# One load moved up in GpSimd's order: the experts' output weights in a fused attention and mixture-of-experts kernel

## The chip, the core and the metric

The kernel runs on one core of one Trainium2 chip, as one program launched once. A core has five engines that run side by side, each through its own list of instructions in order: TensorE for matrix products (PE in the profile, with its weight loads shown apart as PEld), VectorE (DVE), ScalarE (ACT), GpSimd (POOL) and SyncE (SP). An engine goes on to its next instruction when the semaphores which that instruction waits for have come. Transfers between the chip's main memory and the on-chip memory run on 16 DMA engines. They are issued by an instruction on SP, ACT or POOL, and the issuing engine does not wait for them to land.

The metric is the device time of one execution in microseconds (us), as the median of several runs.

## The reference: what is computed

Four batches of 768 positions with 8 heads of 64 columns go through two stages. The first is a sparse attention: each query sees its neighbours within a window, and 24 block summaries (the maximum of the keys of a block of 32 and the mean of its values). The second is a mixture of four attention experts, of which each position uses two.

```
k_sum = k.reshape(B, H, nb, block, D).max(axis=3)
v_sum = v.reshape(B, H, nb, block, D).mean(axis=3)
...
a = np.exp(scores_all)
a = a / (np.sum(a, axis=-1, keepdims=True) + 1e-09)
v_all = np.concatenate([v, v_sum], axis=2)
return np.matmul(a, v_all).astype(np.float32)
```

```
for e in range(E):
    q = x @ wq[e]
    k = x @ wk[e]
    v = x @ wv[e]
    scores = scale * (q @ k.transpose(0, 2, 1))
    ...
    ye = a @ v @ wo[e]
    for kk in range(K):
        mask = topk[:, :, kk] == e
        out += mask[..., None] * w[:, :, kk:kk + 1] * ye
```

The step of this text is the load of `wo`, the last factor in `a @ v @ wo[e]`.

## The kernel before

The kernel is written as a list of some 770 small steps, made by `make_plan`. Each step has a name, the buffers that it reads and writes, and a function that emits its instructions. No loop and no scheduler sets the order in which they run: a hand-made text, `TABLE` (lines 56 to 110), lists the steps by number. Each entry is a step's number, the engine that runs it (P for TensorE, V, A, G for GpSimd, S for SyncE) and the slots of on-chip buffers that it takes. `emit` walks through the table and emits each step. Since every engine runs its own instructions in the order in which they were emitted, the order of the G entries in the table is GpSimd's order, and so on for each engine. What holds between engines are semaphores alone.

In step names the first digit is the batch. The second is the pair of heads (in the first stage) or the pair of experts (in the second).

First stage, for each of four pairs of heads of a batch:

- `dk`, `dq` (lines 263 and 268) load keys and queries through GpSimd's DMA queue. `dv` (lines 287 to 295) loads the values window by window through SP's queue. `dvs` (line 347) loads them once more by blocks, into the one buffer `vt`, and `tr` (line 355, GpSimd) adds them up to block sums. `hc` (line 300) copies window edges and `ds` (line 363) spreads the sums; both run on GpSimd through the copying helper at line 172, `ds` in places on ScalarE.
- `tk`, `tq` (line 374, TensorE) transpose keys and queries. `kw`, `cq` (ACT or DVE) copy them out. `rk` (line 390, DVE) takes the maximum over blocks, and `ksc` (GpSimd) spreads it into `kw`.
- `sc` (lines 422 and 428, TensorE) are the scores, `ex` (line 435, ACT) their exponentials, `av` (line 445, TensorE) the product with the values, `rc` and `xm` (DVE) the normalisation. `tx`, `hi` and `lo` (lines 471 to 490) transpose the result and split it into two half-precision parts.

Second stage, for each batch:

- `vp` (lines 557 and 560, TensorE) gives the experts' values and the gate's logits. `pp` (line 633) gives queries and keys of one pair of experts.
- `sp` (line 657, TensorE), `es` (line 665, ACT) and `dm` (line 670, GpSimd) are the scores of one block of positions, their exponentials and the causal mask. There are six blocks, 0 to 5, for each pair of experts. `aw` (line 681, TensorE) is the product with the values, in three steps; its first step reads blocks 0, 2 and 4.
- `r2` and `wv` (lines 700 to 707, DVE) weigh it with the gate, `tw` (line 718, TensorE) transposes it, and `ct` copies it into the tile `wT`.
- `op` (line 740, TensorE) multiplies `wT` with the output weights, tile `wo`. `oc` copies the result out of the accumulation banks and `od` stores it.

The output weights are loaded once, by step 146, `dwo`, from 32-bit rows into 16-bit ones:

```
def dwo(e):
    nc.gpsimd.dma_start(out=T["wo"], in_=moe_wo.rearrange("(c e) d n -> (e d) c n", c=2))
R.step("dwo", {"G": 0.72}, [], [wo], dwo, dma=256 * 0.066 / 16)
```

The tile has a buffer of its own that nothing else uses, so this load waits for nothing but its turn on GpSimd. Its first reader is step 222, `op00`, the first `op` step of batch 0. In TensorE's order `op00` follows `sp114`, and `pp101`, `sp111`, `sc210`, `tk23` and `tk22` come behind it.

GpSimd's order around the load is, before the change: `dm013`, `dm010`, `dm015`, `dm014`, `dm011`, `dk300`, `dm000`, `dm012`, `dm002`, `dk210`, `dm003`, `dm001`, `dm005`, `tr300`, `dm004`, `dq210`, `ksc20`, `tr301`, `dm110`, **`dwo`**, `vone1` (five small fills, lines 212 to 216), `hc21`, `dm112`, `hc33`, `hc20`, `dm113`, `dm114`, `dq300`, `dm111`, `dm115`, `hc23`, `tr210`, `ksc23`, `ksc22`, `tr211`, `dm101`.

Of the kernel before, what the change touches and what calls it, by code (L numbers as in the profile page):

```python
# [15 lines left out]
S = 768  # L16
# [55 lines left out]
154,P,6 158,V, 271,V, 159,A, 314,P,2.2 155,V, 156,V, 414,G,0 206,P,0 315,A, 295,P,4.3 166,P,6.0 207,A, 160,V,2.0  # L72
162,V, 161,A, 316,P,0.1.0 167,A, 163,V, 317,P, 416,G, 587,S,0 296,A, 585,S, 168,P,6.0 586,S, 318,V, 171,P,2 588,S,
169,A, 319,V, 299,P,4.0.1 415,G, 300,P, 172,A, 180,P,0 419,S,2 301,V, 320,P,6.6.6 208,G, 181,A, 302,V, 199,G,
452,P,2.0 214,G, 435,P,3.2 321,V, 453,A, 205,G, 177,P,4 303,P,0.7.7 211,G, 579,G,1 448,P,2.1.2 436,A, 322,V, 597,S,0
178,A, 170,G, 431,P,3.0.1 202,G, 183,P,6 304,V, 173,G, 184,A, 174,P,4 417,G,0 449,A, 365,P,6.1 305,V, 179,G, 182,G,
175,A, 433,V, 185,G, 367,P,0.0 589,G, 366,A, 450,V, 432,A, 215,P,0.0.4 368,V, 217,P, 421,S,3 451,A, 216,P, 176,G,
372,P,6.1 218,V, 418,G,2 378,P,2 373,A, 186,P,1.1.0 434,G, 219,V, 188,P, 590,G,1 379,A, 187,P, 369,P,6 189,V,
437,P,4.5 370,A, 190,V, 326,P,2.1.1 438,A, 191,P,6.0 327,V, 456,P,0.1 371,G, 328,A, 423,S,0 192,V, 220,P,4.1 146,G,
426,S, 457,A, 221,V, 439,P,2.4 424,S, 375,P,6 38,G,1 440,A, 384,P,4 425,S, 222,P,0.0 376,A, 338,P,2.2 223,V, 408,G,  # L80
385,A, 381,P,6 339,A, 224,S, 454,P,4.2 374,G, 598,G, 482,P,0.2.0 465,P,1.0.2 382,A, 484,V, 329,P,2 455,A, 406,G,
467,V, 323,P,6 483,A, 331,V, 380,G, 377,G, 330,V, 336,P,4.0 466,A, 324,V, 332,V,0.1 580,G,0 334,V, 333,A, 325,A,
383,G, 228,P,2.2 386,G, 337,A, 335,V, 422,G, 225,P,6.4 229,A, 346,P,4.0 427,G, 226,V, 349,P,0 347,A, 387,P,1.0.2
389,P, 350,A, 227,S, 352,P,6 230,S, 388,P, 353,A, 340,P,4 390,V, 485,G, 469,P,0.1 468,G, 391,V, 607,P,1.1.1 341,A,
459,P,6.1.2 428,G,0 470,V, 608,A, 392,P,2.0 458,P, 393,V, 355,P,4 609,V, 473,P,2.3 356,A, 486,P,0.2 474,A, 442,P,4.0.0
460,V, 354,G, 461,V, 600,S,0 487,A, 348,G, 441,P, 601,S, 342,G, 430,G, 343,P,2 443,V, 471,P,0.0 344,A, 472,A, 444,V,
628,P,6.0 624,P,7.0.0 629,V, 357,G, 490,P,4.1 610,G, 462,P,2.0.0 488,P,0.2 491,A, 345,G, 625,V, 351,G, 611,P,6.1
# [817 lines left out]
```

## Time and profile before

| What | us |
|---|---|
| median of 3 runs | 172.43 (171.61 to 174.34) |
| the profiled execution, its own time | 172.59 |
| its span, first to last instruction | 170.9 |
| TensorE busy, of the span | 147.0 (86%) |
| ScalarE busy | 122.2 (72%) |
| VectorE busy | 113.6 (66%) |
| GpSimd busy | 111.1 (65%) |

The span leaves out 1.69 us of the execution's own time (172.59 - 170.9), which lies before its first and behind its last instruction. The profile's page cuts the span into 40 equal slices of 4.27 us and gives a digit for each engine and slice, the busy share in tenths. The row PEclk gives in the same way the clock that TensorE was granted, and the row DMA the load of the 16 DMA engines. The chain of waits is followed back from the last instruction, at each step to what released it. In a timeline a row gives the start, the duration, the engine, the line, the operation, its tiles and the number of instructions merged into it, and in square brackets how long the engine had been idle and what ended that. The ends of matrix products are modelled, so neighbouring rows of TensorE overlap a little. A letter q behind an engine's name marks its sequencer, which issues transfers.

### The profile page before, as it was taken

How to read it: one execution, taken by the hardware profiler on the slowest of the kernel's cores; microseconds unless marked ns; L12 is line 12 of the kernel's file. 1: busy time of each engine (PE TensorE's matmuls, PEld its weight loads, DVE VectorE, ACT ScalarE, POOL GpSimd, SP SyncE). 2: the span in 40 equal slices, each digit the busy share in tenths (PEclk: the TensorE clock that was granted, in tenths of full speed). 3: DMA queues.
4: the chain of work that ended last, by engine and by line, in shares of the span. 5: the costliest groups of instructions: out<-in, count | busy, mean ns of one | idle time of the engine just before them, and what ended most of it. 6: DMA issues, size and time to landing. Idle time of an engine off the chain costs nothing.

```text
span 170.9 us, 6961 instructions
## 1 busy us (share of the span) xinstructions
PE 147.0 (86%) x2993; PEld 107.9 (63%) x2993; DVE 113.6 (66%) x237; ACT 122.2 (72%) x154; POOL 111.1 (65%) x185
## 2 busy tenths in 40 slices
PE   0099999999999999910799998899999999899795
PEld 0076878777867777810265787865777886466552
DVE  5646899897967598710237688893778777546750
ACT  3058989687759898960069978958989795899650
POOL 7988579997789999999029868508799430116000
PEclk9999999999999999995579999999999999999999
DMA  3999999999899699994730370899910000030546
GB/s 26 225 203 230 164 180 206 204 209 205 176 157 202 120 165 211 218 222 104 98 123 0 141 204 4 109 215 190 351 71 4 4 4 2 4 123 0 203 181 233
DMA packets 44222, 24.31 MB, mean 142 GB/s; under 512 B 33184, under 2 KB 40864, under 8 KB 43808
## 3 DMA queue, kind: packets, MB, share of 16 engines
q1 hardware_dynamic: 35824, 16.27, 42.4%
q0 software_dynamic: 7824, 6.56, 26.0%
q10 hardware_dynamic: 544, 1.05, 1.6%
q8 instruction: 23, 0.38, 1.0%
q14 instruction: 7, 0.06, 0.1%
HBM read 24.13 MB, written 6.29 MB: 178 GB/s over the span
## 4 chain that ended last, share of the span: by engine, by line
PE 64%; DMA 11%; POOL 10%; DVE 6%; issue 3%; SPq 2%; ACT 2%; DVEq 0%; POOLq 0%; ACTq 0%
PE ps L633 12%; PE ps L445 11%; PE ps L740 7%; PE ps L557 6%; DMA vb<-in_v_dram 6%; DMA wo<-in_moe_wo_dram 5%; PE ps L681 5%; PE ps L657 4%; PE ps L374 4%; PE ps L471 3%; PE ps L422 3%; POOL vt L355 3%; POOL a L670 3%; PE ps L312 2%; PE ps L428 2%
## 5 line engine op out<-in xcount | busy, mean ns | idle before, releaser
L665 ACT ACTIVATE a<-ps 128x1024 f16<-128x1024 f32 (+1 forms) x48 | 42.1, 922 | 5.4 <-PE ps L657 5.0
L670 POOL TENSOR_SCALAR_AFFINE_SELECT a<-a 128x256 f16<-128x256 f16 x48 | 18.5, 407 | 30.7 <-ACT a L665 30.1
L435 ACT ACTIVATE aT<-ps 120x768 f32<-120x768 f32 x32 | 25.2, 811 | 8.3 <-PE ps L428 7.2
L445 PE MATMUL ps<-vb,aT 120*64 120x65 f32 x768 | 26.2, 223 | 0.7 <-DVE rec L456 0.4
L445 PEld LDWEIGHTS ps<-vb,aT 120*64 120x64 f32 x768 | 23.9, 138 | 3.6 <-issue 1.1
L172 POOL COPY vb<-vb 32x1408 f32<-32x1408 f32 x14 | 18.8, 1349 | 9.8 <-DMA vt<-in_v_dram 6.4
L633 PE MATMUL ps<-hi,wqk 128*128 128x384 f16 x128 | 24.4, 338 | 0.5 <-issue 0.3
L170 ACT COPY kw<-ps 128x1152 f16<-128x1152 f16 x13 | 14.5, 1134 | 8.4 <-PE ps L374 7.7
L355 POOL TENSOR_TENSOR vt<-vt 120x1024 f32<-120x1024 f32 (+3 forms) x16 | 19.2, 1199 | 1.8 <-DMA vt<-in_v_dram 0.9
L740 PE MATMUL ps<-wo,wT 128*128 128x512 f16 (+1 forms) x50 | 12.7, 391 | 8.8 <-DMA wo<-in_moe_wo_dram 8.8
L390 DVE TENSOR_REDUCE ks<-ps 128x24 f16<-128x768 f16 x16 | 14.9, 948 | 6.5 <-ACT kw L170 3.4
L633 PEld LDWEIGHTS <-wqk 128*128 128x128 f16 x128 | 12.4, 101 | 9.9 <-issue 2.8
L170 ACT CAST qk<-ps 128x768 f16<-128x768 f32 x10 | 8.1, 809 | 13.7 <-PE ps L633 13.7
L490 DVE TENSOR_TENSOR lo<-ps,hi 128x768 f16<-128x768 f32 x16 | 15.2, 954 | 2.1 <-ACT hi L170 1.7
L374 PE MATMUL ps<-idr,kn 100*64 100x100 f16 x256 | 8.9, 219 | 8.4 <-DMA kn<-in_k_dram 8.3
L460 DVE TENSOR_TENSOR x<-ps,rec 128x768 f32<-128x768 f32 x16 | 15.3, 956 | 0.5
L657 PE MATMUL ps<-qk,qk 64*128 64x512 f16 (+3 forms) x128 | 14.9, 311 | 0.7 <-ACT qk L170 0.4
L557 PE MATMUL ps<-wvg,hi 128*128 128x264 f16 x96 | 13.8, 275 | 0.1
L172 DVE COPY ob<-ps 128x1024 f32<-128x1024 f32 (+2 forms) x5 | 4.7, 957 | 13.7 <-PE ps L740 13.7
L374 PEld LDWEIGHTS <-kn 100*64 100x64 f16 x256 | 7.3, 117 | 9.3 <-DVE vb L216 8.2
L740 PEld LDWEIGHTS <-wT 128*128 128x128 f16 x50 | 4.4, 100 | 13.9 <-DMA wo<-in_moe_wo_dram 8.9
L428 PEld LDWEIGHTS <-kw 64*128 64x128 f16 x384 | 10.5, 99 | 2.8 <-issue 0.7
(99 smaller groups left out, 292.0 us busy)
## 6 DMA issues: line engine op xcount, KB each, us to landing
vb<-in_v_dram SPq DMA_DIRECT2D x32, 176.0 KB, 5.7
out_dram<-ob SPq DMA_DIRECT2D x9, 512.0 KB, 3.4
vt<-in_v_dram SPq DMA_DIRECT2D x16, 192.0 KB
kn<-in_k_dram POOLq DMA_DIRECT2D x8, 192.0 KB, 6.2
qn<-in_q_dram POOLq DMA_DIRECT2D x8, 192.0 KB, 5.3
kn<-in_k_dram POOLq DMA_DIRECT2D x4, 384.0 KB, 7.5
qn<-in_q_dram POOLq DMA_DIRECT2D x4, 384.0 KB, 6.5
out_dram<-ob ACTq DMA_DIRECT2D x2, 512.0 KB
```

Of the source, the lines that this page charges most:

```text
L170: nc.scalar.copy(dst, src)
L172: en(e).tensor_copy(dst, src)
L355: en(e).tensor_tensor(y[0:120], x[0:120, 0:w], x[0:120, w:2 * w], AL.add)
L374: nc.tensor.transpose(dst[64 * hp:64 * hp + 64, p * s:p * s + p], src[:, hh + hp, 64 * s:64 * s + 64], idt)
L435: nc.scalar.activation(T["aT"][aT.slot][0:KR], pbank(sc, 2)[0:KR, :, 0:384], AF.Exp, scale=SCALE)
L445: nc.tensor.matmul(pbank(av, 2)[o:o + 64, u, 65 * (2 * (t // 2) + hp):65 * (2 * (t // 2) + hp) + 65], a[0:KR, hp, 64 * t:64 * t + 64], T[" ...
L557: nc.tensor.matmul(p[:, i, 0:264], hi_(ch)[:, cols], T["wvg"][:, ch, :], start=(ch == 0), stop=False, skip_group_check=True)
L633: nc.tensor.matmul(pbank(pp, 2)[:, u, 0:384], T["wqk"][:, cc, ch, j, :], hi_(ch)[:, 384 * u:384 * u + 384], start=(ch == 0), stop=(ch == N ...
L657: nc.tensor.matmul(pbank(sp, 2)[:, ep, c0:c0 + w], T["qk"][qk[1].slot][r, 128 * tj:128 * tj + 128], T["qk"][qk[0].slot][r, n0:n0 + w], sta ...
L665: nc.scalar.activation(a2v(u), pbank(sp, 2)[:, :, 0:ln], AF.Exp, scale=SCALE / (XS * XS))
L670: nc.gpsimd.affine_select(m, m, [[0, 2], [1, 128]], AL.is_ge, 0.0, base=0, channel_multiplier=-1)
L740: nc.tensor.matmul(pbank(op, i1 - i0)[:, ti - i0, 0:n1 - n0], T["wT"][wTs[cc].slot][:, 128 * ti:128 * ti + 128], T["wo"][:, cc, n0:n1], st ...
```

## The change

Entry `146,G` is taken out of its place in the table, behind `dm110` (371) and `220,P`, and put in behind `dm014` (205). GpSimd so issues the load ahead of fifteen entries of its order that it followed before: twelve that compute and the three loads `dk300`, `dk210` and `dq210`, which use the same DMA queue. The order of all other entries, on every engine, stays as it was; the other changed lines of the diff are the same entries with other line breaks.

```
-452,P,2.0 214,G, 435,P,3.2 321,V, 453,A, 205,G, 177,P,4 303,P,0.7.7 211,G, 579,G,1 448,P,2.1.2 436,A, 322,V, 597,S,0
...
-437,P,4.5 370,A, 190,V, 326,P,2.1.1 438,A, 191,P,6.0 327,V, 456,P,0.1 371,G, 328,A, 423,S,0 192,V, 220,P,4.1 146,G,
-426,S, 457,A, 221,V, 439,P,2.4 424,S, 375,P,6 38,G,1 440,A, 384,P,4 425,S, 222,P,0.0 376,A, 338,P,2.2 223,V, 408,G,
...
+452,P,2.0 214,G, 435,P,3.2 321,V, 453,A, 205,G, 146,G, 177,P,4 303,P,0.7.7 211,G, 579,G,1 448,P,2.1.2 436,A, 322,V,
...
+437,P,4.5 370,A, 190,V, 326,P,2.1.1 438,A, 191,P,6.0 327,V, 456,P,0.1 371,G, 328,A, 423,S,0 192,V, 220,P,4.1 426,S,
+457,A, 221,V, 439,P,2.4 424,S, 375,P,6 38,G,1 440,A, 384,P,4 425,S, 222,P,0.0 376,A, 338,P,2.2 223,V, 408,G, 385,A,
```

More of the change, by code (lines that the diff above doesn't have):

```diff
@@ L74 @@
 169,A, 319,V, 299,P,4.0.1 415,G, 300,P, 172,A, 180,P,0 419,S,2 301,V, 320,P,6.6.6 208,G, 181,A, 302,V, 199,G,
-452,P,2.0 214,G, 435,P,3.2 321,V, 453,A, 205,G, 177,P,4 303,P,0.7.7 211,G, 579,G,1 448,P,2.1.2 436,A, 322,V, 597,S,0
-178,A, 170,G, 431,P,3.0.1 202,G, 183,P,6 304,V, 173,G, 184,A, 174,P,4 417,G,0 449,A, 365,P,6.1 305,V, 179,G, 182,G,
-175,A, 433,V, 185,G, 367,P,0.0 589,G, 366,A, 450,V, 432,A, 215,P,0.0.4 368,V, 217,P, 421,S,3 451,A, 216,P, 176,G,
-372,P,6.1 218,V, 418,G,2 378,P,2 373,A, 186,P,1.1.0 434,G, 219,V, 188,P, 590,G,1 379,A, 187,P, 369,P,6 189,V,
@@ L79 @@
-437,P,4.5 370,A, 190,V, 326,P,2.1.1 438,A, 191,P,6.0 327,V, 456,P,0.1 371,G, 328,A, 423,S,0 192,V, 220,P,4.1 146,G,
-426,S, 457,A, 221,V, 439,P,2.4 424,S, 375,P,6 38,G,1 440,A, 384,P,4 425,S, 222,P,0.0 376,A, 338,P,2.2 223,V, 408,G,
-385,A, 381,P,6 339,A, 224,S, 454,P,4.2 374,G, 598,G, 482,P,0.2.0 465,P,1.0.2 382,A, 484,V, 329,P,2 455,A, 406,G,
-467,V, 323,P,6 483,A, 331,V, 380,G, 377,G, 330,V, 336,P,4.0 466,A, 324,V, 332,V,0.1 580,G,0 334,V, 333,A, 325,A,
-383,G, 228,P,2.2 386,G, 337,A, 335,V, 422,G, 225,P,6.4 229,A, 346,P,4.0 427,G, 226,V, 349,P,0 347,A, 387,P,1.0.2
@@ L84 @@
-389,P, 350,A, 227,S, 352,P,6 230,S, 388,P, 353,A, 340,P,4 390,V, 485,G, 469,P,0.1 468,G, 391,V, 607,P,1.1.1 341,A,
+452,P,2.0 214,G, 435,P,3.2 321,V, 453,A, 205,G, 146,G, 177,P,4 303,P,0.7.7 211,G, 579,G,1 448,P,2.1.2 436,A, 322,V,
+597,S,0 178,A, 170,G, 431,P,3.0.1 202,G, 183,P,6 304,V, 173,G, 184,A, 174,P,4 417,G,0 449,A, 365,P,6.1 305,V, 179,G,
+182,G, 175,A, 433,V, 185,G, 367,P,0.0 589,G, 366,A, 450,V, 432,A, 215,P,0.0.4 368,V, 217,P, 421,S,3 451,A, 216,P,
+176,G, 372,P,6.1 218,V, 418,G,2 378,P,2 373,A, 186,P,1.1.0 434,G, 219,V, 188,P, 590,G,1 379,A, 187,P, 369,P,6 189,V,
@@ new lines @@
+437,P,4.5 370,A, 190,V, 326,P,2.1.1 438,A, 191,P,6.0 327,V, 456,P,0.1 371,G, 328,A, 423,S,0 192,V, 220,P,4.1 426,S,
+457,A, 221,V, 439,P,2.4 424,S, 375,P,6 38,G,1 440,A, 384,P,4 425,S, 222,P,0.0 376,A, 338,P,2.2 223,V, 408,G, 385,A,
+381,P,6 339,A, 224,S, 454,P,4.2 374,G, 598,G, 482,P,0.2.0 465,P,1.0.2 382,A, 484,V, 329,P,2 455,A, 406,G, 467,V,
+323,P,6 483,A, 331,V, 380,G, 377,G, 330,V, 336,P,4.0 466,A, 324,V, 332,V,0.1 580,G,0 334,V, 333,A, 325,A, 383,G,
+228,P,2.2 386,G, 337,A, 335,V, 422,G, 225,P,6.4 229,A, 346,P,4.0 427,G, 226,V, 349,P,0 347,A, 387,P,1.0.2 389,P,
@@ L85 @@
+350,A, 227,S, 352,P,6 230,S, 388,P, 353,A, 340,P,4 390,V, 485,G, 469,P,0.1 468,G, 391,V, 607,P,1.1.1 341,A,
 459,P,6.1.2 428,G,0 470,V, 608,A, 392,P,2.0 458,P, 393,V, 355,P,4 609,V, 473,P,2.3 356,A, 486,P,0.2 474,A, 442,P,4.0.0
```

## The prediction

> **What bounds the kernel now.** I read the page's slices first, then its chain of waits.
>
> ```profile
> span 170.9 us, 6961 instructions
> PE   0099999999999999910799998899999999899795
> POOL 7988579997789999999029868508799430116000
> PEclk9999999999999999995579999999999999999999
> PE 64%; DMA 11%; POOL 10%; DVE 6%; issue 3%; SPq 2%; ACT 2%; DVEq 0%; POOLq 0%; ACTq 0%
> ```
>
> TensorE is nine tenths busy nearly everywhere, with one hole in the 18th and 19th slice (72.6 to 81.2 us), and its clock falls right behind that. The question is what the hole is. The list of waits, the two engines' timelines and the chain in time answer it:
>
> ```profile
> PE ps L740 <- DMA wo<-in_moe_wo_dram: 8.8, 1, 8.8
> 73.14 0.47 PE L657 MATMUL ps<-qk,qk 64*128 64x512 f16 x4
> 82.38 1.89 PE L740 MATMUL ps<-wo,wT 128*128 128x512 f16 x4 [8.78 <-DMA wo<-in_moe_wo_dram]
> 72.97 0.73 POOL L520 DMA_DIRECT2D wo<-in_moe_wo_dram  x1
> 72.97 9.37 DMA wo<-in_moe_wo_dram
> ```
>
> GpSimd issues the load at 72.97. TensorE has ended its `sp114` and is at `op00` by 73.60, and waits 8.78 us in program order until the load has landed at 72.97 + 9.37 = 82.34. It is the longest single wait on TensorE in its mid-program.
>
> **The load's new place.** It goes behind four of the five mask steps of the first row below (1.85 us for five, 0.37 each), so it is issued at about 60.47 + 4 x 0.37 = 61.95, and moves up by 11.0 us.
>
> ```profile
> 60.47 1.85 POOL L670 TENSOR_SCALAR_AFFINE_SELECT a<-a 128x256 f16<-128x256 f16 x5
> 62.26 0.71 POOL L263 DMA_DIRECT2D kn<-in_k_dram  x1
> 64.05 0.67 POOL L263 DMA_DIRECT2D kn<-in_k_dram  x1
> 68.12 0.40 POOL L670 TENSOR_SCALAR_AFFINE_SELECT a<-a 128x256 f16<-128x256 f16 x1
> 73.69 0.16 POOL L212 MEMSET vb<- 96x24 f32 x1
> ```
>
> *What is late behind it.* Fifteen entries of GpSimd shift by the issue's 72.97 to 73.69, 0.72 us. From 73.69 on GpSimd stands where it stood, since the same instructions lie before that point. Of the fifteen only one is read at once: `dm004`, the row at 68.12, ends at 68.52, and TensorE's `aw000`, which reads block 4, is the second row of 42 products here:
>
> ```profile
> 68.55 1.45 PE L681 MATMUL ps<-v,a 128*128 128x65 f16 x42
> 72.24 1.07 DVE L172 COPY wT<-ps 128x768 f16<-128x768 f16 x2
> ```
>
> It starts 0.03 us after the mask, so I charge it 0.7 us. Behind `aw000` TensorE's queue holds everything up to `op00`, and `op00` also needs the two copies into `wT`, which VectorE makes after `aw000` and which shift along: they end at 73.31 now, 74.0 then. TensorE reaches `op00` at 73.55 + 0.7 = 74.25. The bounds of this term are 0 (if ScalarE's work ahead of the mask hides it) and 0.73.
>
> *When the load lands.* No row shows it at this place. The nearest are the loads on the same software queue, above all the two `kn` loads that are issued in this stretch now (8.0 in the median), the `wo` load itself (9.4), and a `qn` load on a quiet queue (4.8):
>
> ```profile
> kn<-in_k_dram POOLq DMA_DIRECT2D x2, 384.0 KB, 8.0
> wo<-in_moe_wo_dram POOLq DMA_DIRECT2D x1, 256.0 KB, 9.4
> qn<-in_q_dram POOLq DMA_DIRECT2D x1, 384.0 KB, 4.8
> 64.00:68.00 4.00, 4.00 (x60) 2.90 (x58) 3.63 (x4) 3.90 (x5) 4.00 (x6) 1.00 1.25 209
> ```
>
> So between 61.95 + 4.8 = 66.8 and 61.95 + 9.4 = 71.3; I take 8.0, 70.0. Even the late end is 2.9 us ahead of 74.25: the wait goes entirely.
>
> *Whom the transfer displaces.* At the stretch's 209 GB/s (last number of the window's row), 256 KB are 1.25 us for all that is queued behind. `dk210` lands at 64.05 + 8.0 = 72.1 now, then at 72.1 + 0.72 + 1.25 = 74.0; its reader `tk23` stands at 87.81 now and comes to 77.3 (10.5 earlier, below). Slack is 3.3 us. SP's value loads are delayed as well, but their first readers on GpSimd (`hc33`, `hc23`) come at 76 us and later. This is hidden.
>
> **The clock.** While TensorE waits its granted clock halves, and it works slowly after the wait:
>
> ```profile
> 77.00:78.00 1.00, 0.00 (x0) 0.00 (x0) 0.00 (x0) 0.00 (x0) 1.00 (x2) 0.68 0.73 130
> 82.38:84.27 1.89, 1.89 (x5) 0.73 (x6) 0.00 (x0) 0.00 (x0) 0.00 (x0) 0.50 1.16 177
> 87.40:88.00 0.60, 0.60 (x22) 0.46 (x20) 0.00 (x0) 0.60 (x2) 0.00 (x0) 0.83 0.90 345
> 82.38 1.89 PE ps L740 x4
> 84.27 2.56 PE ps L633 x8
> 91.00 1.32 PE ps L633 x8
> 115.26 0.97 PE ps L740 x4
> ```
>
> The last four rows are of the chain of waits: `op00` took 1.89 where the same four products take 0.97 at 115.26, and `pp101` 2.56 where eight take 1.32 at 91.00. That is 0.92 + 1.24 = 2.16 us. The rest up to about 87.5 (`sp111` and `sc210`, some 1 us in the chain at half clock) can hold at most half of itself more, 0.5; I take 0.24, in all 2.4, with bounds 2.16 and 2.66. Without the wait there is nothing to halve the clock: it held at 1.00 for 3.4 us of idleness here, from 73.6 to 77, and the new gap at `aw000` is 0.7.
>
> The Trainium skill, page "TensorE: Matmul & The Clock Gate", section "Part 1: The HAM clock gate (the "warmup" mystery)", says that an idle window of about 3.4 us halves the clock and about 3.4 us of sustained work restores it. The fall at 77 agrees; the way back does not, since the mean clock rises only within the row from 87.40 on, 5.0 us after the work began. By the page's 3.4 us at half speed the loss would be an estimated 1.7 us, and the sum below 0.7 us smaller; the rows decide.
>
> **The sum.** Span: 170.9 - 8.78 (wait) + 0.7 (`dm004`) - 2.4 (clock) = 160.4. With the 1.69 us around the span (172.59 - 170.9) that is 162.1 us; the profiled execution is 0.16 above the median of the runs (172.43), which I leave out. The gain is 10.5 us, 6%.
>
> **Does it hold to the end?** What used the wait to catch up is next in line: ScalarE and VectorE, idle 11.51 and 11.06 us around it, and GpSimd.
>
> ```profile
> 74.06 1.30 ACT L665 ACTIVATE a<-ps 128x1024 f16<-128x1024 f32 x2
> 86.87 0.80 ACT L170 CAST qk<-ps 128x768 f16<-128x768 f32 x1 [11.51 <-PE ps L633]
> 84.38 1.23 DVE L172 COPY ob<-ps 128x1024 f32<-128x1024 f32 x1 [11.06 <-PE ps L740]
> 80.05 0.77 POOL L268 DMA_DIRECT2D qn<-in_q_dram  x1
> 88.67 0.77 POOL L670 TENSOR_SCALAR_AFFINE_SELECT a<-a 128x256 f16<-128x256 f16 x2 [7.86 <-ACT a L665]
> 94.52 0.66 PE L681 MATMUL ps<-v,a 128*128 128x65 f16 x16
> 103.24 0.77 POOL L670 TENSOR_SCALAR_AFFINE_SELECT a<-a 128x256 f16<-128x256 f16 x2 [1.93 <-ACT a L665]
> 105.54 1.45 PE L681 MATMUL ps<-v,a 128*128 128x65 f16 x42
> ```
>
> ScalarE ends its backlog at 74.06 + 1.30 = 75.36, then 76.1; its next work, the copy behind `pp101`, is ready at 86.87 - 10.4 = 76.5. VectorE is free at 74.0 and `op00` ends at 75.2. Neither is late. GpSimd is: it runs without a gap to 80.82 and begins the row of 88.67 there, only 7.86 us earlier, where TensorE has moved by 10.5. So it is 2.6 us behind its old place relative to TensorE. Its readers have room: `aw110`, the products at 94.52, come to 84.0, and the masks end at 81.6. Further on GpSimd waits 1.93 us at 103.24, which takes the lag down to 0.7 us; the reader at 105.54 has 105.54 - 104.01 = 1.5 us of room. So I let TensorE keep its 10.5 us; the loads for batch 3 are released by TensorE itself and move with it.
>
> **Rivals.**
>
> *GpSimd sets the pace.* If a reader that I have not found stands close behind one of GpSimd's steps between 81 and 93 us, or the block loads for `tr210` land late and stretch them, TensorE keeps only GpSimd's 7.86: 170.9 - 7.86 + 1.69 = 164.7. For it speaks that GpSimd is busy in all the slices of 60 to 80; against it the rooms just counted.
>
> *The load starves at its new place, and nothing is gained.* At 61.95 VectorE is in steady work, at 72.97 it was about to go idle. If GpSimd's transfer could not start beside VectorE, it would begin at VectorE's first long pause, 73.31 + 0.7 = 74.0, and land 9.4 later at 83.4, 1.1 behind 82.34: 172.59 + 1.1 = 173.7, no change by the measurement. The two `kn` loads, issued in just this stretch, landed in 8.0 and took 0.71 and 0.67 to issue, no more than `wo` beside an idle VectorE: that speaks plainly against it. The rule behind it is the Trainium skill's, page "SBUF — State Buffer", the box on the DVE blocking DMA: GpSimd cannot write its transfers' descriptors while VectorE holds a port that both share in certain fast modes. By its example (620 ns alone, 3100 ns beside such a copy) the loss would be an estimated 2.5 us and would stay within the slack of 2.9.
>
> *Slower: the queue is served one load at a time.* All GpSimd loads share one queue. If each load there held up the next for its full 9.4 us, `wo` would land at 71.3, `dk300` at 80.7 and `dk210` at 90.1. TensorE would then wait for keys at `tk23`, in the place of the weights, from 77.3 to 90.1, and lose its clock again: 162.1 + 12.8 + 2.4 = 177.3. It turns into a loss when `dk210` lands behind about 87.8, where its reader stands now. Against it: the two `kn` loads, issued 1.79 us apart, each landed in about 8.0, so they overlapped.
>
> **Chances.** Forecast 0.80, GpSimd's pace 0.13, starved load 0.04, served one by one 0.03. The forecast's own range, from its bounds, is 170.9 - 8.78 + 0 - 2.66 + 1.69 = 161.2 to 170.9 - 8.78 + 0.73 - 1.7 + 1.69 = 162.8 (1.7 for the clock is lower than the rows' end, for products that may overlap otherwise); the spread of the runs of before (from 0.5% below their median to 1.1% above) widens it to 160.8 and 164. The range reaches up to the first rival, 164.8, and leaves out the other two, 7 in 100, and some tail. Two per cent of 172.43, 3.4 us, is about what the measurement of this kernel can tell from no change. Faster: forecast and first rival, 0.93. Same: 0.04. Slower: 0.03.
>
> **What would show it.** Right: no wait of TensorE for `wo`, the issue near 62, its landing before 72, PEclk at 9 throughout, `op00` at about 74.2 in 0.97 us, a gap of about 0.7 us ahead of the second group of 42 products near 68.5, the wait of 7.86 on GpSimd gone. Wrong: a landing behind 74.3, a new wait of TensorE for `kn`, for GpSimd's copies or masks between 77 and 100, or TensorE's row of 105.54 less than 10 us earlier.

## The result, and the profile after

| What | before | after |
|---|---|---|
| median of 5 runs on one chip, us | 173.42 (171.61 to 174.4) | 161.75 (160.23 to 163.68) |
| the profiled execution, us | 172.59 | 163.68 |
| its span, us | 170.9 | 162.0 |

The change makes the kernel faster: the ratio is 0.9345, with an interval of 0.9235 to 0.9455. The forecast was 162.1 us. The ratio is one of means, without executions more than 1.5% above the fastest of their kernel, so it is not quite that of the two medians. The experiments below ran beside runs of the kernel before of their own, with medians of 170.7 to 171.3 us; against those the changed kernel's gain is 9.6 to 10.2 us, where the forecast was 10.5.

The page of the changed kernel, the rows that answer to those shown of before:

```profile
span 162.0 us, 6961 instructions
PE   0099999699993999999999999999999998999795
POOL 6989395999789999598999999019999330235100
PEclk9999999999999999999999999999999999999999
```

TensorE's hole in the 18th and 19th slice is gone and its clock no longer falls there. There are two new, smaller dips, in the 8th slice (28.4 to 32.4 us) and in the 13th (48.6 to 52.7 us), both ahead of the place of the change. GpSimd's idle stretch in the 20th and 21st slice of before is gone, too. The timelines show the load and its reader:

```profile
61.47 0.75 POOL L520 DMA_DIRECT2D wo<-in_moe_wo_dram  x1
70.84 0.40 POOL L670 TENSOR_SCALAR_AFFINE_SELECT a<-a 128x256 f16<-128x256 f16 x1
71.70 1.45 PE L681 MATMUL ps<-v,a 128*128 128x65 f16 x42
76.68 1.04 PE L740 MATMUL ps<-wo,wT 128*128 128x512 f16 x4
77.55 1.46 PE L633 MATMUL ps<-hi,wqk 128*128 128x384 f16 x8
82.65 1.46 PE L633 MATMUL ps<-hi,wqk 128*128 128x384 f16 x8
```

The view of the tile `wo` gives its way from issue to landing in this execution:

```profile
DMA to landing us min/median/max: 4.1/4.1/4.1
```

So it lands at 61.47 + 4.1 = 65.6, eleven microseconds ahead of `op00`, which follows the product before it without a gap (no idle time in brackets). From `op00` to `pp100`, the last two rows of line 633 above counted from 76.68, TensorE takes 5.97 us; in the kernel before it took 90.86 - 82.38 = 8.48.

But `op00` starts at 76.68 and not at the 74.25 forecast, and the gap foreseen ahead of the 42 products at 71.70 is not there. The reason lies further up. The same two places of TensorE's timeline, first of the kernel before, then of the changed one:

```profile
30.50 1.62 PE L445 MATMUL ps<-vb,aT 120*64 120x65 f32 x48 [0.26 <-DVE lo L490]
49.53 0.65 PE L633 MATMUL ps<-hi,wqk 128*128 128x384 f16 x3 [0.30 <-issue]
```

```profile
31.19 1.62 PE L445 MATMUL ps<-vb,aT 120*64 120x65 f32 x48 [1.25 <-DVE lo L490]
52.67 0.65 PE L633 MATMUL ps<-hi,wqk 128*128 128x384 f16 x3 [2.75 <-issue]
```

In the middle of a group of eight products, which waits for no other engine, TensorE stood for 2.75 us in place of 0.30. The view calls such idle time "issue": the engine waited for nothing that the profile shows. The changed kernel's profiled execution was late by 3.14 us at this point, before anything of the change: 0.69 us since 31.19, where TensorE had waited longer for VectorE, and 2.45 us by this wait. Whether that belongs to the change, and what it hides, was the first question to the experiments.

### The profile page after: what moved, and what is told of

Same layout as the page of the kernel before. It is cut to its first block, busy times and chain, and to the rows that moved or that the text cites. A ratio compares the mean times of both kernels' runs of the same rounds, so it can differ in the third digit from the quotient of the medians.

```text
span 162.0 us, 6961 instructions
## 1 busy us (share of the span) xinstructions
PE 144.4 (89%) x2993; PEld 107.5 (66%) x2993; DVE 114.3 (71%) x237; ACT 122.2 (75%) x154; POOL 111.1 (69%) x185
## 3 DMA queue, kind: packets, MB, share of 16 engines
q10 hardware_dynamic: 544, 1.05, 1.7%
## 4 chain that ended last, share of the span: by engine, by line
PE 74%; DVE 7%; DMA 6%; issue 5%; ACT 3%; SPq 2%; POOL 1%; DVEq 0%; POOLq 0%; ACTq 0%
PE ps L633 14%; PE ps L445 12%; PE ps L557 7%; PE ps L681 7%; PE ps L740 7%; PE ps L657 6%; DMA vb<-in_v_dram 6%; PE ps L374 5%; PE ps L471 3%; PE ps L422 3%; PE ps L312 3%; PE ps L428 2%; PE ps L772 2%; PE ps L560 1%; SPq L292 1%
## 5 line engine op out<-in xcount | busy, mean ns | idle before, releaser
L633 PE MATMUL ps<-hi,wqk 128*128 128x384 f16 x128 | 23.1, 326 | 2.9 <-issue 2.7
L633 PEld LDWEIGHTS <-wqk 128*128 128x128 f16 x128 | 11.9, 97 | 11.4 <-issue 3.7
L681 PE MATMUL ps<-v,a 128*128 128x65 f16 x336 | 12.1, 193 | 0.0
L681 PEld LDWEIGHTS <-a 128*128 128x128 f16 x336 | 11.1, 97 | 1.6 <-issue 0.6
L172 POOL COPY vb<-vu 24x768 f32<-24x768 f32 x14 | 11.5, 822 | 0.7
L740 PE MATMUL ps<-wo,wT 128*128 128x512 f16 (+1 forms) x50 | 11.9, 371 | 0.0
```

Of the source, the lines that this page charges most:

```text
L172: en(e).tensor_copy(dst, src)
L633: nc.tensor.matmul(pbank(pp, 2)[:, u, 0:384], T["wqk"][:, cc, ch, j, :], hi_(ch)[:, 384 * u:384 * u + 384], start=(ch == 0), stop=(ch == N ...
L681: nc.tensor.matmul(pbank(av, 2)[:, ep, 65 * ti:65 * ti + 65], a2v(u)[:, ep, o:o + 128], T["v2"][v2.slot][:, tj, 2 * cc + ep, :], start=(tj ...
L740: nc.tensor.matmul(pbank(op, i1 - i0)[:, ti - i0, 0:n1 - n0], T["wT"][wTs[cc].slot][:, 128 * ti:128 * ti + 128], T["wo"][:, cc, n0:n1], st ...
```

## The experiments

**The changed kernel three times more** (no edit), for other profiled executions of it.

> The changed kernel itself, once more, for a second look. The profiled execution of it shows TensorE idle for 2.75 us (ended by issue) ahead of the sixth of eight products of line 633, where the kernel before shows 0.30 us at the same product; both follow a transfer of the instruction queue. If this is a matter of the single execution, the wait comes out at another length here and the span is about 159.3 us plus that wait; if it belongs to the change, it is 2.7 us again and the span 162.0. The mask dm004: if it holds TensorE, as the prediction has it, a gap of about 0.7 us stands ahead of the second group of 42 products of line 681 in an execution with a short wait for issue; if ScalarE or TensorE itself is later there, no gap.

> The changed kernel a third time, for its profile. In nine executions so far, TensorE went on with the sixth of eight products of line 633 between 2.9 and 3.3 us after the instruction queue began a transfer of 16,384 bytes, if that began late enough to matter (46.7 us or later from the start of the span). The same is expected here, whatever the wait; from op00 to the end of the span 85.3 us; and ahead of the second group of 42 products of line 681 a gap of up to 0.7 us if the wait for issue is under 0.5 us, none if it is over 1 us.

> The changed kernel a fourth time, for its profile, with the same expectations as the third: 2.9 to 3.3 us from the instruction queue's transfer to the sixth of eight products of line 633, 85.3 us from op00 to the end of the span, and a gap ahead of the second group of 42 products of line 681 only where the wait for issue is short.

The first gave 161.1 us (ratio 0.9427, 0.9344 to 0.951, against its own runs of the kernel before) and a span of 160.4; the others spans of 159.9 and 159.4. From `op00` to the end of the span the four executions took 85.29, 85.28, 85.28 and 85.27 us: behind `op00` they are the same to 0.02 us, and all that differs lies ahead of it. The wait for issue at line 633 was 2.75, 1.65, 0.00 and 1.20 us (the second execution had one more, of 1.10 us at 63.38), so it belongs to the execution and not to the change. Where it was absent, in the third, TensorE's timeline shows the gap that was forecast, with GpSimd's masks as its end; at 0.96 us it is above the 0.7 expected at most:

```profile
68.48 0.33 PE L681 MATMUL ps<-v,a 128*128 128x65 f16 x5
69.76 1.30 PE L681 MATMUL ps<-v,a 128*128 128x65 f16 x37 [0.96 <-POOL a L670]
74.59 1.04 PE L740 MATMUL ps<-wo,wT 128*128 128x512 f16 x4
```

In the fourth, TensorE was late by its wait for issue of 1.20 us, and the same 42 products ran without a gap from 69.14. A load's 0.75 us on GpSimd costs TensorE something only if TensorE is not later itself. Of the 0.96 us, no more than that 0.75 can be the load's; the rest is lateness that GpSimd had already.

**The mask ahead of the block sums.** The mask `dm004` (176) is emitted ahead of `tr300` (589), otherwise the changed kernel.

```
-182,G, 175,A, 433,V, 185,G, 367,P,0.0 589,G, 366,A, 450,V, 432,A, 215,P,0.0.4 368,V, 217,P, 421,S,3 451,A, 216,P,
-176,G, 372,P,6.1 218,V, 418,G,2 378,P,2 373,A, 186,P,1.1.0 434,G, 219,V, 188,P, 590,G,1 379,A, 187,P, 369,P,6 189,V,
+182,G, 175,A, 433,V, 185,G, 367,P,0.0 176,G, 589,G, 366,A, 450,V, 432,A, 215,P,0.0.4 368,V, 217,P, 421,S,3 451,A, 216,P,
+372,P,6.1 218,V, 418,G,2 378,P,2 373,A, 186,P,1.1.0 434,G, 219,V, 188,P, 590,G,1 379,A, 187,P, 369,P,6 189,V,
```

> The changed kernel with one more entry moved: the mask dm004 goes ahead of the block sums tr300, so that the load's issue cannot make it late. If the mask's lateness of 0.7 us is on TensorE's path, this is 0.7 us faster than the changed kernel (about 161.0 against 161.7, 0.930 of the kernel before); if it is not, the two agree (0.934).

160.99 us, a ratio of 0.9442 (0.939 to 0.9494), beside 161.1 and 0.9427 for the changed kernel in the same comparison: no difference that these runs can tell. In its profile, with no wait for issue upstream, the 42 products run without a gap:

```profile
68.86 1.45 PE L681 MATMUL ps<-v,a 128*128 128x65 f16 x42
73.83 1.04 PE L740 MATMUL ps<-wo,wT 128*128 128x512 f16 x4
```

In the third execution of the changed kernel `op00` started at 74.59. Between these two executions that is the 0.7 us expected, but in the medians it drowns in the spread that the waits for issue make. The expectation of 0.7 us in the time was not met, that of the place was. The edit also takes `tr300` (2.35 us) from ahead of the mask, so it shows that the mask ends the gap, and not how much of the gap is the load's.

**The wait filled with work.** In the kernel before, TensorE runs 38 products ahead of `op00`, into the bank that `op00` overwrites.

```
+for _ in range(38 if (b, i0) == (0, 0) else 0):
+    nc.tensor.matmul(pbank(op, 2)[:, 0, :], T["wT"][wTs[0].slot][:, 0:128],
+                     T["wT"][wTs[0].slot][:, 0:512], start=True, stop=True)
 for ti in range(i0, i1):
     for cc in range(2):
```

> The kernel before, with 38 products of 128x512 (about 0.216 us each, 8.2 us in all) run by TensorE ahead of op00, into the bank that op00 then overwrites: they fill most of its wait for the output weights without shortening it. If the falling clock costs 2.4 us behind the wait, as the prediction has it, the time is 2.4 us below the kernel before (ratio 0.986), with op00 at 82.4 in about 1 us and the clock at 1.00; if the loss is what 3.4 us of half speed make, 1.7 us (0.990); if the other engines, and not TensorE, set the pace behind the wait, the time does not change (1.000).

Its timeline of TensorE:

```profile
73.15 8.38 PE L739 MATMUL ps<-wT 128*128 128x512 f16 x38
81.40 1.02 PE L743 MATMUL ps<-wo,wT 128*128 128x512 f16 x4
82.26 1.46 PE L633 MATMUL ps<-hi,wqk 128*128 128x384 f16 x8
87.36 1.46 PE L633 MATMUL ps<-hi,wqk 128*128 128x384 f16 x8
108.61 0.33 PE L445 MATMUL ps<-vb,aT 120*64 120x65 f32 x3 [0.84 <-issue]
```

From `op00` to `pp100` it takes 87.36 - 81.40 = 5.96 us, as in the changed kernel, with the granted clock at 1.00: the clock's loss of 2.5 us is all of the difference to 8.48, and the other engines have no part in it. Yet the time was 171.77 us, a ratio of 1.007 (1.0032 to 1.0108): no gain, and 0.7% of a loss. The profile shows 0.84 us of a new wait for issue, 24 transfers of the instruction queue in place of 23, and 3.4 us behind the last product in place of 1.9. The extra instructions seemed to cost something of their own, which the next run was to take out.

> The experiment with filled wait once more, with 128 products of 128x144 (about 62 ns each, 8.0 us in all) in place of 38 of 128x512. In the first form the stretch from op00 to the products pp100 took 5.96 us, as in the changed kernel (5.97), against 8.48 in the kernel before, so 2.5 us came back; but the time was 1.2 us above the kernel before: TensorE waited 0.84 us for issue at 108.6, the instruction queue made 24 transfers in place of 23, the last at 163.3, and the end behind the last product took 3.4 us in place of 1.9. If that is the instruction queue, whose transfers of 16,384 bytes fall on other places of the program with 76 instructions more, 256 instructions more (each pair a weight load and a product) are one whole transfer and leave the places behind it as they are: the time is then 2.5 us below the kernel before (ratio 0.985). If warm products cost the rest of the kernel something in another way, the ratio is 1.00 or above again.

```
+for _ in range(128 if (b, i0) == (0, 0) else 0):
+    nc.tensor.matmul(pbank(op, 2)[:, 0, 0:144], T["wT"][wTs[0].slot][:, 0:128],
+                     T["wT"][wTs[0].slot][:, 0:144], start=True, stop=True)
 for ti in range(i0, i1):
     for cc in range(2):
```

168.93 us, a ratio of 0.9894 (0.9838 to 0.995): the gain appears. Its interval holds the 2.5 us expected and the 2.0 of the next run. From `op00` to the end it took 85.43 us, within 0.2 of the changed kernel. The run with 38 products took 87.80 us there, 2.4 more: 0.84 is its wait for issue and 1.5 the longer end. That a program made longer by a whole transfer of instructions keeps its pace, and one made longer by a part of a transfer does not, is the reading that led to this run, and it fits; the two runs also differ in the size and number of their products, and no run separates the two.

**The kernel before once more** (no edit).

> The kernel before once more, for a second profile of it. TensorE's wait for wo (8.78 us), the stretch from op00 to pp100 (8.48 us) and the fall of the clock come back within 0.3 us if they belong to the kernel; the waits for issue (0.30 us at the sixth of eight products of line 633, 0.50 us at 104.48) come at other lengths if they belong to the single execution.

This one execution took 173.89 us. The wait for `wo` came back (8.61 us), the waits for issue were 1.20 us at line 633 and none near 104. The stretch from `op00` to `pp100` took 7.93 us and not 8.48: the expectation of 0.3 us failed. Stretches cut where the records of the granted clock change say why. The columns are the stretch, its length, the busy time of PE, PEld, DVE, ACT and POOL, then the clock, the DMA share and GB/s. First the kernel before in its first profile, then in this one:

```profile
73.60:77.37 3.77, 0.00 (x1) 0.00 (x0) 0.00 (x0) 1.76 (x3) 3.39 (x9) 1.00 1.01 209
77.37:82.38 5.01, 0.00 (x0) 0.00 (x0) 0.00 (x0) 0.00 (x0) 3.38 (x5) 0.50 0.49 86
82.38:87.61 5.23, 5.23 (x24) 2.20 (x26) 1.23 (x1) 0.74 (x2) 0.00 (x0) 0.50 0.65 147
```

```profile
76.35:78.72 2.37, 0.00 (x1) 0.00 (x0) 0.00 (x0) 1.76 (x3) 2.11 (x6) 1.00 1.14 232
78.72:84.97 6.25, 0.00 (x1) 0.01 (x1) 0.00 (x0) 0.00 (x0) 4.29 (x6) 0.50 0.68 117
84.97:88.96 3.99, 3.99 (x12) 1.59 (x12) 1.22 (x1) 0.00 (x0) 0.00 (x0) 0.50 0.57 88
```

The half clock lasts the same 10.24 us in both (5.01 + 5.23; 6.25 + 3.99), but the work meets it at another point: 5.23 us of work at half speed lose some 2.6, 3.99 us some 2.0, and the stretches were longer than the changed kernel's by 2.51 and 1.96. From `op00` to the end this execution took 87.22 us, 1.94 more than the changed kernel: here the clock is all of the difference.

**Half the way.** The load goes just behind `dm004`, five entries up.

```
-175,A, 433,V, 185,G, 367,P,0.0 589,G, 366,A, 450,V, 432,A, 215,P,0.0.4 368,V, 217,P, 421,S,3 451,A, 216,P, 176,G,
+175,A, 433,V, 185,G, 367,P,0.0 589,G, 366,A, 450,V, 432,A, 215,P,0.0.4 368,V, 217,P, 421,S,3 451,A, 216,P, 176,G, 146,G,
...
-437,P,4.5 370,A, 190,V, 326,P,2.1.1 438,A, 191,P,6.0 327,V, 456,P,0.1 371,G, 328,A, 423,S,0 192,V, 220,P,4.1 146,G,
+437,P,4.5 370,A, 190,V, 326,P,2.1.1 438,A, 191,P,6.0 327,V, 456,P,0.1 371,G, 328,A, 423,S,0 192,V, 220,P,4.1
```

> The kernel before with the load moved up by five entries in place of fifteen, to just behind the mask dm004, so that it is issued at about 68.5 us, behind both key loads and ahead of dq210. If the loads of GpSimd's queue are served in order, it lands behind dk210 (72.5), with 256 KB at 209 GB/s at about 74, and TensorE, there at 73.55, waits 0.5 to 1 us; the clock holds and the time is about 1 us above a load without any wait and about the changed kernel's, 161 to 163. If a load needs its 9.4 us wherever it is issued, it lands at 77.9: a wait of 4.3 us, the clock falls, and the time is 167 to 169. If it needs the 4.1 us of the changed kernel, it lands at 72.6 and there is no wait.

163.7 us, a ratio of 0.9583 (0.951 to 0.9656): 2.6 us above the changed kernel's 161.1 in the same comparison, and above the 161 to 163 expected.

```profile
49.16 0.61 POOL L172 CAST wqk<-a 128x512 f16<-128x512 f32 x1 [2.61 <-DMA a<-in_moe_wk_dram]
70.44 0.75 POOL L520 DMA_DIRECT2D wo<-in_moe_wo_dram  x1
70.54 1.30 PE L681 MATMUL ps<-v,a 128*128 128x65 f16 x37 [1.05 <-POOL a L670]
76.94 1.04 PE L740 MATMUL ps<-wo,wT 128*128 128x512 f16 x4 [1.21 <-DMA wo<-in_moe_wo_dram]
77.81 1.46 PE L633 MATMUL ps<-hi,wqk 128*128 128x384 f16 x8
```

The load landed 6.4 us after its issue and left 1.21 us of the wait, without a fall of the clock. That is near the forecast by the queue's order (0.5 to 1 us), and not that by 9.4 us or by 4.1. In the same trace `dk210` lands at 74.17, so the load came 2.7 us behind the one that it was queued after. But in the fourth execution of the changed kernel, with neither key load ahead of it, the load also took 6.4 us, so that the queue's order set the landing here is not shown. TensorE waited 1.05 us for `dm004` although the load stands behind that mask: GpSimd had waited 2.61 us for another weight load at 49.16 and was late by itself. The mask has next to no room at all. This profile also holds a wait for issue of 1.08 us, at 97.10.

**The idle place.** The load goes ahead of `hc12` (248), where GpSimd was idle.

```
-248,G, 151,P,6.0.0 285,V, 412,S, 411,S, 308,V, 41,G,4 286,P,0.4.4 203,P,2 287,A, 152,V, 153,V, 251,P,4.1 204,A, 288,V,
+146,G, 248,G, 151,P,6.0.0 285,V, 412,S, 411,S, 308,V, 41,G,4 286,P,0.4.4 203,P,2 287,A, 152,V, 153,V, 251,P,4.1 204,A, 288,V,
...
-437,P,4.5 370,A, 190,V, 326,P,2.1.1 438,A, 191,P,6.0 327,V, 456,P,0.1 371,G, 328,A, 423,S,0 192,V, 220,P,4.1 146,G,
+437,P,4.5 370,A, 190,V, 326,P,2.1.1 438,A, 191,P,6.0 327,V, 456,P,0.1 371,G, 328,A, 423,S,0 192,V, 220,P,4.1
```

> The load moved up much further, to just behind the copy hc13 of batch 1, where GpSimd stands idle for 1.49 us at 41.85 in the kernel before, waiting for a value load. Its issue of 0.72 us then lies in idle time and it is far ahead of TensorE's need. If all that counts is that the load lands ahead of 73.5 us, the time is that of the changed kernel or, without the issue ahead of the mask dm004, up to 0.7 us less: ratio 0.930 to 0.938. If the transfer of 256 KB in that stretch holds up the value load that GpSimd waits for there, by up to 1.25 us (256 KB at 209 GB/s), GpSimd's unbroken run up to the mask dm004 ends later by as much and TensorE waits there: 1 us slower than the changed kernel.

161.2 us, a ratio of 0.9423 (0.9362 to 0.9484): the changed kernel's time. The load took 10.0 us from its issue at 42.68, and nobody waited for that; GpSimd's next copy followed at 43.40 without a wait. Neither the 0.7 us less nor the 1 us more can be told from this interval.

**More work for GpSimd.** Six fills of 0.52 us on a tile that nobody reads there, behind the masks of step `dm115`, in the changed kernel.

```
 nc.gpsimd.affine_select(m, m, [[0, 2], [1, 128]], AL.is_ge, 0.0, base=0, channel_multiplier=-1)
+for _ in range(6 if (b, cc, u) == (1, 1, 5) else 0):
+    nc.gpsimd.memset(T["zz"], 0.0)
```

> The changed kernel with six more fills of 0.52 us on GpSimd (3.1 us), on a tile that nobody reads there, behind the mask dm115, where GpSimd in the profile of the changed kernel runs without a gap from 66.76 to 94.8. Readers have room: the masks dm102 and dm103 end at 95.80 and the products that read them start at 96.69. If GpSimd has only that 0.9 us to give, TensorE waits about 2.2 us ahead of its third group of 42 products of line 681 and the kernel is 2.2 us (1.4% of the changed kernel) slower; if GpSimd is far from the path, nothing changes.

The edit put the fills at two places, behind `dm115` and behind `dm105`, since the function reads `cc` only when it runs. The time was 168.09 us, a ratio of 0.986 (0.9809 to 0.9912), 6 to 7 us above the changed kernel: TensorE waited for masks for 4.06 us, and its clock fell for 6.83. With the first place alone (`cc` bound in the function's arguments):

> The six fills on GpSimd once only, behind dm115. In the run before this one they stood at two places, behind dm115 (3.44 us) and behind dm105 (3.43 us), and TensorE waited for masks 0.56 us at 96.25 and 3.50 us at 100.36, its clock fell for 6.8 us, and the kernel was 6.7 us slower. With the first place alone, the mask dm103 would end there at about 97.3 and the product that reads it was wanted at about 96.3: TensorE waits about 1.0 us, its clock holds, and the kernel is about 1.0 us slower than the changed one. The room by the first estimate (0.9 us) says 2.5 us slower; that GpSimd is far from the path says no change.

164.88 us, a ratio of 0.9637 (0.9453 to 0.9822), 3.3 and 3.8 us above the two single executions of the changed kernel in the same comparison (161.57 and 161.09). The interval is too wide to tell the 1.0 us expected from 2.5, so the profile has to. The profile, POOL's fills first and then TensorE's rows with new waits:

```profile
81.95 3.44 POOL L673 MEMSET zz<- 128x512 f16 x6
90.03 0.35 PE L428 MATMUL ps<-qT,kw 64*128 64x64 f16 x12 [0.60 <-POOL kw L172]
96.30 1.45 PE L683 MATMUL ps<-v,a 128*128 128x65 f16 x32 [0.55 <-POOL a L670]
101.75 0.35 PE L428 MATMUL ps<-qT,kw 64*128 64x64 f16 x12 [1.16 <-POOL kw L172]
```

The three waits add up to 2.31 us, and from `op00` to the end the kernel takes 87.89 us, 2.61 more than without the fills. Of 3.44 us on GpSimd, 0.83 were hidden, in an execution in which TensorE was not late by itself (it had waited 1.31 us for `dm004` at 69.73). That is the room of the first estimate, 0.9 us; my second one, which looked at the masks alone, forgot `ksc` (the copies into `kw`), where the largest of the three waits stands.

## Why the prediction was right

- *The wait of 8.78 us goes entirely*: right in all four executions. The landing was expected 8.0 us after the issue, between 4.8 and 9.4; it took 4.1 in the first, 4.2 to 6.4 in the others. The lower bound was too high, without effect on the time: the load had 6 us and more in hand in place of 2.9.
- *The issue moves to 61.95*: 61.47 in the profile after, and 0.75 us of GpSimd's time for 0.72.
- *0.7 us for the mask*: the mechanism is right, shown by the third execution (a gap of 0.96) and by the run with the mask moved (none). The size was right in part by luck. The gap is GpSimd's whole lateness and not the load's alone: the run with the load half way has 1.05 without the load ahead of the mask. And in each of the three traces with a gap five products of the group run ahead of it, so the mask was not wanted at the start of the 42, where the prediction counted its 0.03 us, but a little later. The 0.7 was also charged to every execution; it falls away where TensorE is late by itself, as in three of four.
- *2.4 us for the clock*: 2.5, shown by the filled wait, where the work from `op00` to `pp100` was the same and the clock held. It is not a constant of the kernel: the second profile of before lost 1.96, below the rows' bound of 2.16. The 1.7 that the range reaches down to was not seen behind this wait.
- *TensorE keeps what it gains to the end*: right. Behind `op00` the changed kernel takes 85.29 us and the kernel before 88.50. Of these 3.21, 2.51 are the clock, 0.50 a wait for issue at 104.48 in the profile of before, and 0.2 remain unexplained. In the second profile of before the clock's 1.96 cover the whole.
- *GpSimd has room of 1.5 us and more*: too much. It had 0.8 in the one profile that measures it, so the first rival (GpSimd sets the pace) was nearer than its argument made it; the room was still enough: behind `op00` no execution of the changed kernel shows a wait of TensorE for GpSimd.
- *The starved load* did not occur: beside VectorE's work (busy for 3.13 of the 4.13 us) the load was issued in 0.75 us and landed in 4.1, faster than the 9.4 beside an idle VectorE. The Trainium skill's rule for it (page "SBUF — State Buffer", the box on the DVE blocking DMA) leaves no mark here; it speaks of certain fast modes of VectorE, and no run shows which mode VectorE worked in, so it is not refuted either. The slower rival did not occur either: `dk210` landed 8.6 us after its issue, at 75.3, in front of its reader at 79.61.
- *Two slips in the range*: 0.5% below its lower end and 1.1% above its upper end are 160.4 and 164.6, not 160.8 and 164; and the first rival's time is 164.7 by its own sum, not 164.8, which the upper end of 164 does not reach. Neither touches the forecast.

In sum for the third execution, which had no wait for issue: 170.88 - 8.78 + 0.99 (of which 0.96 the mask) - 3.21 (behind `op00`) = 159.88, and its span is 159.87. The forecast of the span was 160.4. What brought the first profile to 162.0 is above all the wait for issue, which the prediction did not have; the median lies between. The mechanism was right; that the median came within 0.4 us of the forecast is partly luck, since executions of the changed kernel spread from 160.23 to 163.68.

## What to carry to other kernels

A long wait of the bounding engine for one load costs its length and what the clock loses behind it, and gives back both if the load's issue is moved up far enough; how far cannot be read from one landing time alone, since this one load took between 4.1 and 10.0 us by where it was issued. An early issue is not free: it delays what stands behind it on its engine, and the price is the room of the tightest reader there, which a few fills of known length measure quickly. Compare profiled executions at a common mark (here, from `op00` to the end) before reading a difference of a microsecond into a change.

## What the runs showed of the hardware

**TensorE's waits for issue follow transfers on the instruction queue.** Those at line 633 come behind transfers of 16,384 bytes there. From the trace's records, in microseconds:

```
execution                  transfer starts   sixth product starts   difference   wait
changed, fourth            47.13             50.12                  2.99         1.20
before, first              46.67             49.53                  2.86         0.30
changed, second            47.38             50.27                  2.89         1.65
fills at two places        47.48             50.42                  2.94         1.20
filled wait, 128 products  47.32             50.34                  3.02         1.47
idle place                 48.40             51.60                  3.20         2.29
before, second             49.13             52.27                  3.14         1.20
changed, first             49.36             52.67                  3.31         2.75
```

TensorE goes on 2.9 to 3.3 us after the transfer starts, whatever the wait. In the five other executions the transfer started between 44.0 and 45.6, and there was no wait. The six further waits for issue of 0.50 to 1.11 us (at 104.48, 97.10 and 108.61 in the first profile of before, the load half way and the filled wait with 38 products, and near 63.4 in three executions) end 2.5 to 2.9 us after such a transfer's start. (The expectations of the third and fourth spoke of nine executions; seven had such a wait by then.) The transfer shares the DMA engines with value loads, at a share of 1.35 in the idle place's wait. That it is the fetch of TensorE's own instructions is the reading that fits all thirteen, with the filled waits; no run takes the loads away to prove it. The Trainium skill, page "Runtime: NRT & Kernel Launch", section "Instruction fetch mechanics", has instructions fetched in blocks of 16 KiB, 256 instructions each, which agrees with the size of these transfers. It calls their cost "mostly hidden"; that agrees for most of the 23 transfers of an execution, and not for this one, with waits of 0.30 to 2.75 us in eight of thirteen executions.

**The clock moves on a fixed grid.** The half-speed stretches of the records last 10.24 us (twice, above), 6.83 (fills at two places) and 3.41 (below): three, two and one times 3.41. The stretches at full speed ahead of them fit the same step: 61.44 us in the first profile of before is 18 of them, 37.55 in the run with the idle place 11. The Trainium skill, page "TensorE: Matmul & The Clock Gate", section "Part 1: The HAM clock gate (the "warmup" mystery)", has a free-running window of 3413 ns, which agrees. Its advice (same page, section "Why this matters for your kernels") against idle gaps over some 3 us was too lax here: a wait of 2.29 us for issue was enough in the run with the idle place,

```profile
49.31:51.60 2.29, 0.00 (x1) 0.00 (x1) 0.35 (x1) 0.00 (x0) 1.76 (x2) 1.00 1.35 146
51.60:52.55 0.95, 0.95 (x19) 0.50 (x20) 0.20 (x1) 0.00 (x0) 0.00 (x0) 1.00 1.34 180
52.55:55.96 3.41, 3.41 (x52) 2.58 (x45) 1.72 (x2) 2.98 (x3) 2.62 (x2) 0.50 1.40 200
```

where the window that ended at 52.55 had TensorE idle for 2.29 of its 3.41 us, while the 2.75 us in the first profile of the changed kernel left the clock at 1.00: counted in steps of 3.41 from where its clock rose first (16.82), a window ends at 50.95, inside the wait from 49.92 to 52.67, and neither side holds more than 1.72 us of it. A window at 0.50 that is full of work, as the last row's, loses an estimated 1.7 us.
